# Folding a chunk's w_out with phi in the column group beside the logits' products, one chunk later

## The chip, the core and the metric

The kernel runs on one core of a Trainium2 chip. The metric is the device time of one execution in microseconds (us); the time of a kernel is the median of its runs.

## What is computed

Three layers follow each other: attention over 4 batches of 512 local and 32 global tokens (8 heads of 64), a gated feed-forward layer of 512 to 1536 to 512 (`moe_`), and a soft mixture of experts (`moe2_`). The change concerns the second layer's last matrix and the first product of the third:

```python
def _moe_ref(x, w_gate, w_val, w_out):
    g = x @ w_gate
    silu = g * (1.0 / (1.0 + np.exp(-g)))
    val = x @ w_val
    return silu * val @ w_out

def _moe2_ref(x, phi, w1, w2):
    logits = x @ phi
    d = softmax over the tokens; c = softmax over the slots
    slot_input = d.T @ x
    ...
```

The kernel never forms the second layer's output. With h = silu * val, the logits are h @ (w_out @ phi), so each 128 rows of w_out are multiplied with phi (512 x 32) once, and the 128 x 32 result is what the logits' products need.

## The kernel before, in words

The 17 tiles of 128 tokens (2176 tokens) are cut into blocks, and the blocks into two groups. Group 1 (`G1`) holds three blocks of 512 tokens, group 2 (`G2`) one of 384 and one of 256. The 1536 inner features are 12 chunks of 128 (`NFC` = 12). In group 1 the loop of line 847 goes over the chunks c, and in each over the three blocks: `gate(0, c, blk)` (line 605), then `val(0, c, blk)` (line 617). Each is one group of 12 TensorE products of 128 x 128 weights with 512 columns (`mm3`, line 594: four slices of x, three products each for the high and low parts). After a gate, ScalarE takes a tanh (line 612, tile `u`) and VectorE multiplies (line 613). After a val, VectorE multiplies again (line 622) and transposes (line 625). Between these, VectorE, ScalarE and GpSimd prepare the weights of the next chunk (lines 127 to 176).

Small pieces of work are put between the products by hand. `at(k, f)` (line 585) enters a piece f at step k, and `mm3` calls the pieces of a step after every third product. A chunk has `S1` = 24 steps: chunk c has the steps 24c to 24c + 23, its first gate the first four, its first val the next four, and so on. Pieces are issued in the engines' program order where they stand, so a piece on TensorE stands in front of all later products. The pieces of chunk c:

- `wprime(c)` (line 627) has three. Its `a` turns the chunk's 128 x 512 of w_out with four transposes into PSUM (`pwt`, line 634); ScalarE copies them out (`woT`, line 637). Its `b`, the fold, multiplies the four turned slices with the four slices of phi. Each of the four products gives 32 output rows, and they go to the four groups of 32 rows of `pwp` (line 642), one each, as four separate partial results. VectorE copies all 128 rows out (`ws`, line 647). Its `e`, the turn back, is one product `pws` (line 651) whose contraction over 128 rows with four stacked unit matrices (`istack`) adds the four partial results and turns them, to 128 x 32; ScalarE copies it out (`wp`, line 652).
- `logits_piece(0, [c - 1])` (line 656) has three products, one for each block: the folded weights of chunk c - 1 (128 x 32) with the block's `u` of 512 columns (line 669). Block 0, 1 and 2 write to output rows 0 to 31, 32 to 63 and 64 to 95 of one bank (`L`). Rows 96 to 127 stay free. They are added up over the chunks.

A product of 32 output rows uses one of four groups of 32 columns of TensorE's array, a product that contracts 32 rows one of four groups of 32 rows. The profile writes the part that an instruction uses as rows*columns: 128*128 is the whole array, 128*32 one column group, 32*128 one row group. A product of plain 32-bit floats is recorded as two MATMUL and two LDWEIGHTS, here called its two passes.

Before, the pieces stand at these steps of chunk c: the logits of chunk c - 1 at 5 (in the middle of the first val), `a` at 9, the fold at 12, the turn back at 15; for chunk 0 the three are five steps later. The `u` tiles live in two pools (line 793), one for even and one for odd chunks, of three buffers each. PSUM has three buffers for the groups of products (`ps_mm`), one for the transposes and one shared by `pwp` and `pws` (`ps_w`).

Of the kernel before, what the change touches and what calls it, by code (L numbers as in the profile page):

```python
# [23 lines left out]
NC = DM // P  # L24
# [12 lines left out]
def window(i):  # L37

    if i == 0:
        return 0, "A", 0  # L40
    m, k = divmod(i - 1, 3)
    return (4 * m, 4 * m + 2, 4 * m + 3)[k], "ABC"[k], m
# [3 lines left out]
def attention_moe_soft_moe_kernel(  # L46
# [15 lines left out]
    nc = tc.nc  # L62
    FF = w_gate.shape[1]
    NFC = FF // P
    NS = phi.shape[1]
# [19 lines left out]
    istack = cpool.tile([P, NS], F32, name="istack")  # L85
# [3 lines left out]
    phi_sb = cpool.tile([P, NC, NS], F32, name="phi_sb")  # L89
# [4 lines left out]
    for i, (_, n) in enumerate(BLOCKS):  # L94
        pool = x2pool if i in GROUPS[-1] else x1pool
        t = pool.tile([P, 2 * NC * n * P], F32R, name=f"x{i}")
        t = t.rearrange("p (a c n) -> p a c n", a=2, c=NC)
# [80 lines left out]
    def prep_some(n=1):  # L178
        for _ in range(min(n, len(prep))):
            prep.pop(0)()  # L180
# [86 lines left out]
    pw = ps_sc.tile([P, 512], F32, tag="sc", name="pw")  # L267
# [21 lines left out]
    for g in (0, 1, 3, 2):  # L289
# [7 lines left out]
        for r in range(3):  # L297
# [3 lines left out]
            k = window(first)[1]  # L301
# [277 lines left out]
    def cols(blk):  # L579
        return BLOCKS[blk][1] * P  # L580
# [4 lines left out]
    def at(k, f):  # L585
        plan.setdefault(k, []).append(f)
# [18 lines left out]
    def gate(g, c, blk, fill=True):  # L605
        n = cols(blk)
        pg = ps_mm.tile([P, 512], F32, tag="mm", name=f"pgate{g}_{c}_{blk}")
        mm3(pg, wchunk[c], 0, blk, fill)

        w, bufs = usize[c % 2]  # L610
        u = us[c, blk] = upools[c % 2].tile([P, w], F32, tag="u", name=f"u{g}_{c}_{blk}", bufs=bufs)
        nc.scalar.activation(u[:, :n], pg[:, :n], AF.Tanh, scale=0.5)  # L612
        nc.vector.scalar_tensor_tensor(  # L613
            out=u[:, :n], in0=u[:, :n], scalar=1.0, in1=pg[:, :n], op0=ALU.add, op1=ALU.mult
        )

    def val(g, c, blk, fill=True):
        n = cols(blk)
        pv = ps_mm.tile([P, 512], F32, tag="mm", name=f"pval{g}_{c}_{blk}")
        mm3(pv, wchunk[c], 1, blk, fill)  # L620
        u = us[c, blk]
        nc.vector.scalar_tensor_tensor(  # L622
            out=u[:, :n], in0=u[:, :n], scalar=0.5, in1=pv[:, :n], op0=ALU.mult, op1=ALU.mult
        )
        nc.vector.transpose(out=hT[blk][:, c], in_=u[:, :n])  # L625

    def wprime(c):

        d = {}

        def a():
            pt = ps_w.tile([P, NC, P], F32, tag="wt", name=f"pwt{c}")
            for cc in range(NC):
                nc.tensor.transpose(pt[:, cc], wo[c][:, cc * P : cc * P + P], ident)
            wo.pop(c)
            t = d["t"] = wtmp.tile([P, NC, P], F32, tag="woT", name=f"woT{c}")
            nc.scalar.activation(t, pt, AF.Copy)  # L637

        def b():
            pp = ps_w.tile([P, P], F32, tag="wp", name=f"pwp{c}")  # L640
            for j in range(NC):
                nc.tensor.matmul(
                    pp[32 * j : 32 * j + 32], phi_sb[:, j], d["t"][:, j],
                    start=True, stop=True, skip_group_check=True,
                )
            d["s"] = wtmp.tile([P, P], F32, tag="ws", name=f"ws{c}")
            nc.vector.tensor_copy(d["s"], pp)

        def e():
            pw = ps_w.tile([P, NS], F32, tag="wp", name=f"pws{c}")  # L650
            nc.tensor.matmul(pw, d["s"], istack, start=True, stop=True)
            nc.scalar.activation(wp[c], pw, AF.Copy)

        return a, b, e

    def logits_piece(g, cs, blks=None):

        group = GROUPS[g]
        per = 4 // len(group)

        def f():
            if g not in Lps:
                Lps[g] = ps_L.tile([P, 512], F32, tag="L", name=f"L{g}")
            for c in cs:
                for bi, blk in enumerate(group):
                    if blk not in (blks or group):
                        continue
                    cg, n = bi * per + c % per, cols(blk)
                    nc.tensor.matmul(  # L669
                        Lps[g][32 * cg : 32 * cg + 32, :n], wp[c], us.pop((c, blk))[:, :n],  # L670
                        start=(c < per), stop=(c >= NFC - per), skip_group_check=True,
                    )

        return f
# [164 lines left out]
    def w_fetch(i):  # L839
        c = i - NFC  # L840
        if c >= NFC:
            return
        w = wchunk[i] = ring_tile(i, f"wr{c}")
        nc.sync.dma_start(w.bitcast(F32), wkept[c])

    S1, S2 = 2 * NC * len(G1), 2 * NC * len(G2)
    for c in range(NFC):

        if c > 0:
            at(S1 * c + 5, logits_piece(0, [c - 1]))  # L850
        for k, f in zip((9, 12, 15), wprime(c)):
            at(S1 * c + k + (5 if c == 0 else 0), f)
        if c + 2 >= NFC:
            w_fetch(c + 2)
        for bi, blk in enumerate(G1):
            if c + 1 < NFC:
                w_prep(3 * (c + 1) + bi)
            if c > 0:
                gate(0, c, blk)
            prep_some(2)  # L860
            val(0, c, blk)
            prep_some(3)
# [34 lines left out]
    t = epool[0].tile([P, 4096], F32, name="dr0", tag="e0")  # L897
    t = [t[:, 512 * k : 512 * k + 512] for k in range(5)]
# [17 lines left out]
    k = base + 30  # L916
# [98 lines left out]
    d, a, b, top, turned, tokens, sums, NJ = part_end(2, Ls, [Ls], [place["rB"]])  # L1015
# [42 lines left out]
    t = dpool.tile([P, 4 * NF], F32, tag="Ts", name="sT")  # L1058
    nc.gpsimd.memset(t[:, : 5 * E * DG], 0.0)  # L1059
    t = t[:, : 5 * E * DG].rearrange("p (c k) -> p c k", c=5)  # L1060
# [5 lines left out]
    for h, hs in enumerate((H1, H2)):  # L1066
        psi = ps_mm.tile([P, DM // 2], F32, tag="mm", name=f"psi{h}")
        for c in range(NFC):
# [3 lines left out]
                start=(c < 4), stop=(c >= NFC - 4), skip_group_check=True,  # L1072
# [8 lines left out]
    for c in range(NC):  # L1081
        nc.tensor.matmul(
            psTi[:, c], (si0, si)[c // 2][:, c % 2 * P : c % 2 * P + P], istack,
            start=True, stop=True, skip_group_check=True,
# [48 lines left out]
    for k in range(3, 2 * E):  # L1133
# [4 lines left out]
        if side == 0:  # L1138
            t = epool[slot > 0].tile([P, 4096], F32, name=f"f{slot}", tag=f"e{slot}")
# [17 lines left out]
    for i in range(5, NEARLY):  # L1157
        t = epool[1].tile([P, 4096], F32, name=f"ob{i}", tag=f"e{i}")
# [121 lines left out]
```

## Time and profile before

| | |
|---|---|
| three runs | 537.39, 538.96, 540.86 us; median 538.96 |
| the profiled execution, its own time | 538.02 us |
| its span (first to last instruction) | 536.1 us |
| TensorE (PE) busy | 501.7 us, 94% of the span |
| VectorE (DVE), ScalarE (ACT), GpSimd (POOL) busy | 304.1, 181.8, 97.3 us |
| mean granted TensorE clock | 0.985 of full speed |

PE is TensorE's matmuls, PEld its weight loads, SP the engine that issues most transfers. A matmul's record is longer than the time to the next one's start, since they are pipelined: distances from start to start are what is read below. The lines of the tables belong to the program before; in the changed program the same code stands two or three lines lower from `wprime` on.

### The profile page before, as it was taken

The numbers are of one execution on the slowest core, as the hardware profiler recorded it, in microseconds if no ns is written. First come the engines' busy times: TensorE is split into PE (matmuls) and PEld (weight loads), VectorE is DVE, ScalarE is ACT, GpSimd is POOL, SyncE is SP. The second block draws the span as 40 slices with busy tenths as digits, with TensorE's granted clock in tenths as the row PEclk, the third lists the DMA queues.
The fourth block names the chain that finished last, engine by engine and source line by source line (L and its number), as shares of the span: only waits on it lengthen the run. The fifth ranks groups of instructions, "written<-read, shape, count | busy, mean of one in ns | idle before, by whom it ended". The sixth has DMA issues, their size and how long they took to land.

```text
span 536.1 us, 12836 instructions
## 1 busy us (share of the span) xinstructions
PE 501.7 (94%) x5274; PEld 373.9 (70%) x5274; DVE 304.1 (57%) x801; ACT 181.8 (34%) x550; POOL 97.3 (18%) x137
## 2 busy tenths in 40 slices
PE   5879999999999999999999999999999999779982
PEld 3668787887777777777777777785699997433631
DVE  7556988867776677677667666362243434521012
ACT  5758898873323223223223221130101112110011
POOL 7853665421201001001011110000000000100000
PEclk9899999999999999999999999999999999989997
DMA  8996886603653444344444463142199996869996
GB/s 217 303 272 179 234 265 166 172 5 98 216 174 122 163 150 156 138 137 158 137 150 168 141 231 134 43 158 81 60 398 384 415 388 205 320 211 351 348 360 194
DMA packets 61922, 109.94 MB, mean 205 GB/s; under 512 B 3752, under 2 KB 47784, under 8 KB 59944
## 3 DMA queue, kind: packets, MB, share of 16 engines
q1 hardware_dynamic: 61864, 109.13, 61.0%
q8 instruction: 41, 0.67, 0.5%
q14 instruction: 17, 0.14, 0.1%
HBM read 88.93 MB, written 20.19 MB: 204 GB/s over the span
## 4 chain that ended last, share of the span: by engine, by line
PE 70%; issue 13%; ACT 7%; DVE 4%; DMA 3%; SPq 1%; DVEq 0%; ACTq 0%
PE pval L598 22%; PE pgate L598 22%; PE sc L342 4%; PE ppT L372 3%; PE T L760 3%; PE psh L1101 3%; PE o L386 2%; DMA f<-in_w_dram 2%; ACT p L363 2%; PE pso L1171 2%; PE L L669 1%; PE gs L447 1%; SPq L876 1%; ACT woT L637 1%; PE pg L479 1%
## 5 line engine op out<-in xcount | busy, mean ns | idle before, releaser
L598 PE MATMUL pval<-x,w 128*128 128x512 f32 x432 | 112.3, 400 | 0.0
L598 PE MATMUL pgate<-x,w 128*128 128x512 f32 x432 | 109.8, 399 | 0.0
L598 PEld LDWEIGHTS pval<-x,w 128*128 128x128 f32 x432 | 79.4, 188 | 28.1 <-issue 11.6
L598 PEld LDWEIGHTS pgate<-x,w 128*128 128x128 f32 x432 | 79.5, 189 | 16.7
L613 DVE SCALAR_TENSOR_TENSOR u<-u,pgate 128x512 f32<-128x512 f32 (+2 forms) x60 | 36.5, 608 | 84.7 <-ACT u L612 84.6
L612 ACT ACTIVATE u<-pgate 128x512 f32<-128x512 f32 (+2 forms) x60 | 31.8, 530 | 128.3 <-PE pgate L598 106.5
L622 DVE SCALAR_TENSOR_TENSOR u<-u,pval 128x512 f32<-128x512 f32 (+2 forms) x60 | 36.4, 607 | 48.6 <-PE pval L598 48.5
L172 POOL TENSOR_TENSOR w<-wb,w 128x512 fp32r<-128x512 f32 x24 | 31.2, 1301 | 179.9 <-ACT w L171 179.8
L363 ACT ACTIVATE p<-sm,nm 128x128 f32<-128x128 f32 x128 | 49.4, 393 | 0.0
L598 PE MATMUL pgate<-x,wr 128*128 128x384 f32 (+1 forms) x288 | 49.3, 314 | 0.0
L598 PEld LDWEIGHTS pgate<-x,wr 128*128 128x128 f32 x288 | 43.5, 188 | 8.1 <-issue 7.4
L598 PE MATMUL pval<-x,wr 128*128 128x384 f32 (+1 forms) x288 | 48.5, 314 | 0.0
L598 PEld LDWEIGHTS pval<-x,wr 128*128 128x128 f32 x288 | 43.1, 189 | 7.0 <-issue 7.0
L171 ACT ACTIVATE w<-wb 128x512 fp32r<-128x512 f32 x24 | 15.2, 632 | 86.7 <-issue 51.4
L342 PE MATMUL sc<-kS,qB 128*64 128x128 f32 x512 | 34.0, 280 | 7.9 <-ACT pG L466 3.1
L342 PEld LDWEIGHTS sc<-kS,qB 128*64 128x64 f32 x512 | 28.4, 138 | 13.3 <-issue 8.2
L353 DVE CUSTOM_DVE_ANT_0 sm<-sc,masks 128x128 f32<-128x128 f32 x128 | 28.7, 286 | 11.0 <-PE sc L342 9.4
L157 DVE SCALAR_TENSOR_TENSOR wb<-wv,wb 128x512 f32<-128x512 f32 x36 | 25.6, 712 | 3.5
L1059 POOL MEMSET sT<- 128x1440 f32 x1 | 1.3, 1297 | 139.1 <-PE pTT L1038 139.1
L625 DVE STREAM_TRANSPOSE hT<-u 128x512 f32<-128x512 f32 x36 | 25.6, 712 | 1.3
L143 DVE SCALAR_TENSOR_TENSOR wb<-raw,wb 128x512 uint32<-128x512 uint32 x36 | 25.3, 704 | 1.1
L363 ACT ACTIVATION_READ_ACCUMULATOR p<-sm,nm 128x1 f32 x128 | 24.7, 193 | 0.0
(211 smaller groups left out, 679.3 us busy)
## 6 DMA issues: line engine op xcount, KB each, us to landing
e<-in_w_dram SPq DMA_DIRECT2D x7, 2048.0 KB, 12.8
w_d<-w SPq DMA_DIRECT2D x24, 512.0 KB, 2.6
wr<-w_d SPq DMA_DIRECT2D x12, 1024.0 KB, 6.2
f<-in_w_dram SPq DMA_DIRECT2D x10, 1024.0 KB, 12.0
raw<-in_wgate_dram SPq DMA_DIRECT2D x12, 512.0 KB, 3.6
raw<-in_wval_dram SPq DMA_DIRECT2D x12, 512.0 KB, 4.0
raw<-in_wout_dram SPq DMA_DIRECT2D x12, 512.0 KB, 3.5
kS<-in_kS_dram SPq DMA_DIRECT2D x7, 736.0 KB, 6.6
```

What stands on the lines that cost most here:

```text
L143: nc.vector.scalar_tensor_tensor(out=d["t"], in0=d["raw"][:, :, 0], scalar=29, in1=d["t"], op0=ALU.logical_shift_right, op1=ALU.bitwise_or,)
L157: nc.vector.scalar_tensor_tensor(out=w, in0=d["v"], scalar=F64_NORMAL, in1=w, op0=ALU.is_ge, op1=ALU.mult)
L172: nc.gpsimd.tensor_tensor(out=wl, in0=w, in1=wh, op=ALU.subtract)
L342: nc.tensor.matmul(sc[64 * (i % 2) : 64 * (i % 2) + 64, i // 2], qb[:, hp, blk], kS[n][:, hp, 32 * s0 : 32 * s0 + 128], start=True, stop=T ...
L353: nc.vector.tensor_tensor_reduce(out=sm[:, bp], in0=sc[:, bp], in1=masks[:, 4 * tp + bp], scale=-SCALE, scalar=3e38, op0=ALU.add, op1=ALU.min,
L363: nc.scalar.activation(d["p"][hp][:, bp], d["sm"][hp][:, bp], AF.Exp, bias=d["nm"][:, hp, bp : bp + 1], scale=-1.0, accum_out=d["rs"][:, b ...
L372: nc.tensor.transpose(pt[:, bp], d["p"][hp][:, bp], ident)
L598: nc.tensor.matmul(ps[:, :n], w[:, 2 * k + a, cc * P : cc * P + P], xt[b][:, cc], start=(cc == 0 and i == 0), stop=(cc == NC - 1 and i == 2),)
L612: nc.scalar.activation(u[:, :n], pg[:, :n], AF.Tanh, scale=0.5)
L613: nc.vector.scalar_tensor_tensor(out=u[:, :n], in0=u[:, :n], scalar=1.0, in1=pg[:, :n], op0=ALU.add, op1=ALU.mult)
L622: nc.vector.scalar_tensor_tensor(out=u[:, :n], in0=u[:, :n], scalar=0.5, in1=pv[:, :n], op0=ALU.mult, op1=ALU.mult)
L625: nc.vector.transpose(out=hT[blk][:, c], in_=u[:, :n])
```

## The change

```diff
@@ wprime
         def b():
+            r = slice(3 * NS, 4 * NS)
             pp = ps_w.tile([P, P], F32, tag="wp", name=f"pwp{c}")
             for j in range(NC):
                 nc.tensor.matmul(
-                    pp[32 * j : 32 * j + 32], phi_sb[:, j], d["t"][:, j],
-                    start=True, stop=True, skip_group_check=True,
+                    pp[r], phi_sb[:, j], d["t"][:, j],
+                    start=(j == 0), stop=(j == NC - 1), skip_group_check=True,
                 )
             d["s"] = wtmp.tile([P, P], F32, tag="ws", name=f"ws{c}")
-            nc.vector.tensor_copy(d["s"], pp)
+            nc.vector.tensor_copy(d["s"][r], pp[r])
 
         def e():
+            r = slice(3 * NS, 4 * NS)
             pw = ps_w.tile([P, NS], F32, tag="wp", name=f"pws{c}")
-            nc.tensor.matmul(pw, d["s"], istack, start=True, stop=True)
+            nc.tensor.matmul(pw, d["s"][r], istack[r], start=True, stop=True)
             nc.scalar.activation(wp[c], pw, AF.Copy)
@@ the loop over the chunks of group 1
+        last = c == NFC - 1
+        f, fold, back = wprime(c)
+        at(S1 * c + (14 if c == 0 else 9), f)
+        k = S1 * c + 13 if last else S1 * (c + 1) + 3
         if c > 0:
-            at(S1 * c + 5, logits_piece(0, [c - 1]))
-        for k, f in zip((9, 12, 15), wprime(c)):
-            at(S1 * c + k + (5 if c == 0 else 0), f)
+            at(k, logits_piece(0, [c - 1]))
+        at(k, fold)
+        at(k + 4, back)
```

The fold's four products now all write to output rows 96 to 127, the group that the logits' products leave free, and add up there, one after the other. VectorE copies 32 rows instead of 128. The turn back contracts those 32 rows alone, in one row group. The transposes stay where they were. The fold of chunk c moves to step 3 of chunk c + 1, right behind the logits of chunk c - 1, which also go there (before: step 5 of chunk c); the turn back follows at step 7. The last chunk has its logits (of chunk 10), fold and turn back at its own steps 13, 13 and 17. In chunk 1 the fold of chunk 0 stands alone, with no logits before it. The number of products is the same.

On TensorE, from the first gate of chunk 2 to its last: `pgate_2_0` is the gate of chunk 2, block 0. Before:

```order
L598 MATMUL pgate_2_0_2792<-x_82,w_2686 128x512 x12
L598 MATMUL pval_2_0_2813<-x_82,w_2686 128x512 x6
L669 MATMUL L_2670<-u_1_0_2655,wp_2533 32x512
L669 MATMUL L_2670<-u_1_1_2711,wp_2533 32x512
L669 MATMUL L_2670<-u_1_2_2764,wp_2533 32x512
L598 MATMUL pval_2_0_2813<-x_82,w_2686 128x512 x6
L598 MATMUL pgate_2_1_2840<-x_83,w_2686 128x512 x6
L634 MATMUL pwt_2847<-ident,wb_2767 128x128 x4
L598 MATMUL pgate_2_1_2840<-x_83,w_2686 128x512 x6
L598 MATMUL pval_2_1_2868<-x_83,w_2686 128x512 x3
L642 MATMUL pwp_2872<-woT_2852,phi_sb 32x128 x4
...
L651 MATMUL pws_2888<-istack,ws_2877 128x32
```

The same stretch of the changed program:

```order
L598 MATMUL pgate_2_0_2778<-x_82,w_2682 128x512 x12
L672 MATMUL L_2791<-u_0_0_2357,wp_2532 32x512
L672 MATMUL L_2791<-u_0_1_2472,wp_2532 32x512
L672 MATMUL L_2791<-u_0_2_2501,wp_2532 32x512
L644 MATMUL pwp_2795<-woT_2699,phi_sb 32x128 x4
L598 MATMUL pval_2_0_2810<-x_82,w_2682 128x512 x12
L654 MATMUL pws_2823<-istack,ws_2800 128x32
L598 MATMUL pgate_2_1_2837<-x_83,w_2682 128x512 x6
L634 MATMUL pwt_2844<-ident,wb_2753 128x128 x4
L598 MATMUL pgate_2_1_2837<-x_83,w_2682 128x512 x6
L598 MATMUL pval_2_1_2865<-x_83,w_2682 128x512 x12
```

The logits' three products and the fold's four now stand in one place between the first gate and the first val, the logits those of two chunks ago; the turn back stands behind the first val.

On VectorE, around the first gate of chunk 3 (`wb` are the weights in preparation, `ws` is the fold's copy). Before:

```order
L157 SCALAR_TENSOR_TENSOR wb_2916<-wv_2917,wb_2916 128x512
L613 SCALAR_TENSOR_TENSOR u_3_0_2954<-u_3_0_2954,pgate_3_0_2941 128x512
L137 TENSOR_SCALAR wb_2957<-raw_2894 128x512
L143 SCALAR_TENSOR_TENSOR wb_2957<-raw_2894,wb_2957 128x512
L622 SCALAR_TENSOR_TENSOR u_3_0_2954<-u_3_0_2954,pval_3_0_2962 128x512
```

After:

```order
L157 SCALAR_TENSOR_TENSOR wb_2903<-wv_2904,wb_2903 128x512
L649 COPY ws_2949<-pwp_2944 32x128
L613 SCALAR_TENSOR_TENSOR u_3_0_2951<-u_3_0_2951,pgate_3_0_2928 128x512
L137 TENSOR_SCALAR wb_2954<-raw_2881 128x512
L143 SCALAR_TENSOR_TENSOR wb_2954<-raw_2881,wb_2954 128x512
L622 SCALAR_TENSOR_TENSOR u_3_0_2951<-u_3_0_2951,pval_3_0_2959 128x512
```

The copy, which stood in front of the line 622 of block 1, now stands in front of the line 613 of block 0. The orders of GpSimd and of the transfers are the same as before.

## Rows read from the trace of the kernel before

**Rows 1.** The page, part 4: the chain that ended last, shares by engine.
```profile
PE 70%; issue 13%; ACT 7%; DVE 4%; DMA 3%; SPq 1%; DVEq 0%; ACTq 0%
```

**Rows 2.** Stretch, its us, busy us (instructions) of PE, PEld, DVE, ACT, POOL; clock, DMA, GB/s.
```profile
146.20:352.00 205.80, 204.02 (x986) 151.99 (x986) 136.88 (x224) 52.87 (x104) 25.44 (x20) 1.00 0.43 149
```

**Rows 3.** Timeline of PE, chunk 4: start us, us, line, out<-in, count [idle <-releaser].
```profile
196.11 1.56 PE L598 MATMUL pval<-x,w 128*128 128x512 f32 x6
197.60 1.06 PE L669 MATMUL L<-u,wp 128*32 128x512 f32 x6
198.59 1.67 PE L598 MATMUL pval<-x,w 128*128 128x512 f32 x6
200.10 1.55 PE L598 MATMUL pgate<-x,w 128*128 128x512 f32 x6
...
203.32 0.86 PE L598 MATMUL pval<-x,w 128*128 128x512 f32 x3
204.36 0.43 PE L642 MATMUL pwp<-woT,phi_sb 128*32 128x128 f32 x8 [0.18 <-ACT woT L637]
...
206.92 0.32 PE L651 MATMUL pws<-istack,ws 128*128 128x32 f32 x2
207.08 3.04 PE L598 MATMUL pgate<-x,w 128*128 128x512 f32 x12
209.95 2.96 PE L598 MATMUL pval<-x,w 128*128 128x512 f32 x12
212.75 2.96 PE L598 MATMUL pgate<-x,w 128*128 128x512 f32 x12
215.55 1.57 PE L598 MATMUL pval<-x,w 128*128 128x512 f32 x6
```

**Rows 4.** The same timeline, chunk 0 and chunk 11.
```profile
127.85 2.33 PE L598 MATMUL pval<-x,w 128*128 128x512 f32 x9
...
135.34 2.95 PE L598 MATMUL pgate<-x,w 128*128 128x512 f32 x12
...
338.89 0.86 PE L598 MATMUL pval<-x,w 128*128 128x512 f32 x3
...
345.24 2.96 PE L598 MATMUL pval<-x,w 128*128 128x512 f32 x12
```

**Rows 5.** Who waited for whom on PE, 126 to 352 us: total us, times, longest.
```profile
PE pwp L642 <- ACT woT L637: 1.7, 9, 0.2
```

**Rows 6.** Timeline of PE in the attention: one unit's scores.
```profile
62.68 1.09 PE L342 MATMUL sc<-kS,qB 128*64 128x128 f32 x16
```

**Rows 7.** Line 342 (the scores): ns min/median/max, first and last start, shape.
```profile
L342 PE MATMUL sc<-kS,qB x512: 269/273/418, 6.7 to 109.5; 128*64 128x128 f32 x171
```

**Rows 8.** Line 669 (logits, group 2), records under way between 394.62 and 394.65 us.
```profile
L669 PE MATMUL L<-u,wp x6: 380/404/510, 394.4 to 394.6; 128*32 128x256 f32 x4, 128*32 128x384 f32 x2
```

**Rows 9.** Timeline around a product with 64 contracted rows (line 707), PE.
```profile
446.83 0.88 PE L598 MATMUL pval<-x,wr 128*128 128x256 f32 x6
447.63 0.91 PE L707 MATMUL LB<-xa,istack 64*128 64x384 f32 x2
448.47 0.64 PE L598 MATMUL pval<-x,wr 128*128 128x256 f32 x3
448.95 0.52 PE L598 MATMUL pgate<-x,wr 128*128 128x256 f32 x3
```

**Rows 10.** The chain in order of time: start us, us; a group of 256 columns.
```profile
427.76 1.43 PE pgate L598 x12
```

**Rows 11.** Timeline of DVE around the first gate of chunk 5.
```profile
215.06 0.69 DVE L157 SCALAR_TENSOR_TENSOR wb<-wv,wb 128x512 f32<-128x512 f32 x1
216.38 0.69 DVE L613 SCALAR_TENSOR_TENSOR u<-u,pgate 128x512 f32<-128x512 f32 x1 [0.62 <-ACT u L612]
...
219.73 0.69 DVE L622 SCALAR_TENSOR_TENSOR u<-u,pval 128x512 f32<-128x512 f32 x1 [1.59 <-PE pval L598]
```

**Rows 12.** Timeline of ACT at the same place.
```profile
215.75 0.60 ACT L612 ACTIVATE u<-pgate 128x512 f32<-128x512 f32 x1 [4.12 <-PE pgate L598]
```

## The prediction

> **What bounds the kernel now.** I read the chain of waits first, by engine: 70% of the span is TensorE [rows 1]. In a table of stretches, group 1 from chunk 1 on (146.2 to 352 us) has TensorE busy 204.0 of 205.8 us at the full granted clock, 1.00 of 2.4 GHz, while VectorE is busy 137 and ScalarE 53 [rows 2]. So in this stretch time is the sum of what TensorE issues; other engines matter only where TensorE waits for them. In the list of who waited for whom, TensorE waits for one thing there: the fold for ScalarE's copy of the transposes, 1.7 us in nine places [rows 5].
>
> Then the timeline of one chunk. A group of 12 products with nothing between them takes 2.80 us from start to start (209.95 to 212.75, and 212.75 to 215.55), 0.233 a product [rows 3]. Each piece put between products costs what its group takes beyond that:
> - the logits: 196.11 to 200.10 is 3.99, so 1.19 us;
> - fold and turn back: the 24 products from 203.32 to 209.95 take 6.63 against 5.60, so 1.03 us. Of this the turn back is 0.23: 0.16 from 206.92 to 207.08, and 0.07 by which the next group is longer than 2.80. The fold is the other 0.80, with its wait of 0.18.
>
> **What is removed.** Nine chunks fold with such a wait, so 9 x 1.03 = 9.3 us. Chunk 11 has none: 24 products from 338.89 to 345.24 take 6.35, so 0.75 [rows 4]. Chunk 0 takes 7.49 for the 27 products from 127.85 to 135.34, 1.19 over 6.30; about 0.1 of that I leave to the transposes just ahead, so 1.1. Chunk 1, not shown, I put between, at 1.0. Sum 12.1 us. The transposes and the logits' own 1.19 us stay, whatever their step: both places interrupt the same stream.
>
> **What is added: the fold beside the logits.** Do the fold's eight passes run while the logits' six do? The scores of the attention show how a chain runs in one column group: 16 passes of 128 columns, eight in each of two groups of 64 columns, stand in 1.09 us [rows 6]. A record lasts 0.27 [rows 7], so the last starts 0.82 after the first: 0.117 a pass, and eight of them 0.94 us, with the other group's eight beside them. That column groups also keep their own pace is seen where logits of 384 and of 256 columns stand together: at 394.62 to 394.65 all four passes of 256 columns have begun, but only two of the four with 384 [rows 8]; the short ones' second passes did not wait for the long ones' first. From the logits' first start to the next product are 0.99 us (197.60 to 198.59) [rows 3]. The fold, issued seventh some hundredths later, needs 0.94 plus the way out, so it sticks out by 0 to 0.07; I take 0.04. Eleven places, 0.4 us.
>
> In chunk 1 the fold of chunk 0 stands alone, in one column group: 0.94 for its passes. What entering and leaving another form of tile costs I read at a product that contracts 64 rows [rows 9], against 0.119 a product of 256 columns there (1.43 for 12) [rows 10]. It begins 0.09 late (446.83 plus six products is 447.54, it starts at 447.63); from its start to the next product are 0.84, of which its two passes of 384 columns take some 0.68 (six times 0.117 is 0.70, a little less without the first weights); and the three products behind take 0.48 instead of 0.36, 0.12 more. So 0.09 + 0.16 + 0.12 = 0.37 beside the streaming. The lone fold costs 0.94 + about 0.3 = 1.2 us.
>
> **What is added: the turn back in a row group.** Today it uses the whole array like its neighbours and costs 0.23. With 32 contracted rows it is a tile of another form than the products on both sides, and no row shows such a product with so few columns. From below: 0.37 for changing form twice plus two passes of 32 columns, a quarter of 0.117 each, is 0.43. From above: 0.37 plus all that it costs today is 0.60. I take 0.54, nearer the upper end, since its second weights of 128 columns cannot be covered by a pass as short as 0.03, as the second weights of the 384-column pass can. Twelve times 0.54 is 6.5 us, bounds 5.2 to 7.2.
>
> The Trainium skill, "TensorEngine Tiling (Array Packing)", Key Properties, says that a change of tiling mode drains TensorE. By that rule the turn back gets dearer by the change, and the trace agrees: 0.09 in and 0.12 out at [rows 9]. Without it the turn back would stay at 0.23, a rival below.
>
> **What hides the rest.** VectorE's copy of the fold: at the first gate of chunk 5 VectorE has finished its weight preparation at 215.75 and waits until 216.38 for the tanh [rows 11]. After the change the logits and fold start where that gate ends, about 215.6, and end near 216.6; the copy follows by about 217.0, and the turn back comes behind the next 12 products, at about 219.4. Margin some 2.4 us. The wait also queues behind the copy on VectorE the multiplication of line 613, which waits for the tanh anyway. The tanh (215.75 to 216.35 [rows 12]) must now wait until the logits have read its buffer, so it starts near 216.6, 0.9 later, and line 613 with it; the val's multiplication that follows on VectorE today waits 1.59 for TensorE [rows 11], which takes this up. The PSUM buffer that line 613 frees is wanted again two groups later, over 5 us. If these covers failed, each us would count twelve times. The transposes' copy, for which the fold waits today, is now 18 of a chunk's 24 steps old, some 14 us: that wait goes, and nothing else is late there. No transfer moves, on no queue. Everything behind group 1 is started by TensorE's progress, so I let the whole gain pass to the end.
>
> **Sum.** 0.4 + 1.2 + 6.5 = 8.1 added, 12.1 removed: 4.0 us less. The profiled execution took 538.02 (span 536.1 and 1.9 around it); it becomes 534.0. It is 0.9 below the median of the runs; from the median, 538.96 - 4.0 = 534.9 us, 0.75% less. By the bounds (0 to 0.8 for the overhang, 5.2 to 7.2 for the turn back, 0.2 either way elsewhere) the gain is 2.9 to 5.9, so 533.1 to 536.1.
>
> **Rivals.**
> - *The fold's chain runs behind the logits, not beside them.* All these products use all 128 rows, and the fold is issued last; if its weights had to wait for the logits' products, each of eleven places would pay 0.94 instead of 0.04, 9.9 us more: 534.9 + 9.9 = 544.8, slower. It turns the sign once the fold sticks out by 0.40 (4.0/11 + 0.04). Against it are the independent groups of [rows 6, 8]; for it, that no row shows two lengths of chain. 0.08. In the Trainium skill, "TensorE: Matmul & The Clock Gate", Part 3, weights overlap running products only where the row groups differ; here they don't differ, and by that rule this rival would be the forecast. In [rows 8] second passes start under running ones of the same rows, which is against the rule.
> - *The turn back costs no change of form*, and stays at 0.23: 12 x 0.31 = 3.7 more gained, 531.2. Against it speak [rows 9], though they have 64 rows and long passes. 0.12.
> - *VectorE or ScalarE comes late*, so that the turn back waits half a us in each chunk: +6.0, 540.9. It would need 2.4 us of margin to vanish. 0.05.
> - *The gain is lost behind group 1*, in the last stage's transfers, which TensorE also waits for: 538.5 to 539, no change. The transfers are issued as TensorE frees their buffers, which speaks against it. 0.07.
> - The forecast: 0.68.
>
> **How the numbers follow.** A measurement of this kernel tells about 1%, 5.4 us, from no change. The forecast lies below that; with its bounds and the scatter of the medians (the three runs span 3.5 us) a fifth of it falls over 1% faster: 0.14, and nearly all of the second rival, 0.11: faster 0.25. Slower by over 1% takes 0.05 of the first rival and 0.01 of the third: 0.06. The rest, 0.69, is within 1%. The range of 530.5 to 539.5 holds the forecast, the second and the fourth rival, and leaves out the first and part of the third. The forecast's own range is 533 to 536.5.
>
> **What would show it.** In the timeline after: the logits and the fold side by side, about 1.0 us from the first logits' start to the next product in chunks 2 to 11, near 1.9 if the first rival holds; a lone fold of 0.9 in chunk 1; the turn back delaying TensorE by some 0.54, against 0.23; no wait of the fold for ScalarE; chunk to chunk 19.0 us instead of 19.4 (196.11 to 215.55 [rows 3]). The forecast is wrong if a new wait for VectorE stands before the turn back, or if group 1 ends 4 us sooner and the last instruction does not.

## The result, and the profile after

The changed kernel takes 532.80 us (median of 8 runs, 530.85 to 536.16) against 538.64 (8 runs, 536.88 to 540.86): a ratio of 0.989, 95% interval 0.986 to 0.993, 5.8 us less. A second set of 7 runs gave 532.49 and 0.991 (0.988 to 0.994). The forecast was 534.9 and 0.75% less, in a range of 530.5 to 539.5.

TensorE sets the end as before. The chain of the page after, by engine, the line that answers to [rows 1]:

```profile
PE 88%; DVE 4%; ACT 4%; issue 2%; DVEq 0%; ACTq 0%
```

The 18 points more of TensorE have two sources. In this execution the chain did not pass through the last transfers; in the second trace of the same kernel it did, and there TensorE has 80%. The rest is the share called issue, 2% here and 3% there, against 13% before [rows 1]. Most of that 13% was nine stretches like this one, in which the chain before left TensorE from the logits to the fold of a chunk and came back by way of ScalarE's copy `woT`:

```profile
197.46 5.72 issue
```

What the change did stands in the timeline of TensorE. Chunk 4 after (columns as in [rows 3]; here its first gate, the logits of chunk 2 with the fold of chunk 3, its first val, the turn back):

```profile
188.91 2.96 PE L598 MATMUL pgate<-x,w 128*128 128x512 f32 x12
191.80 0.63 PE L672 MATMUL L<-u,wp 128*32 128x512 f32 x3
191.82 0.62 PE L644 MATMUL pwp<-woT,phi_sb 128*32 128x128 f32 x4
192.25 0.60 PE L672 MATMUL L<-u,wp 128*32 128x512 f32 x3
192.28 0.60 PE L644 MATMUL pwp<-woT,phi_sb 128*32 128x128 f32 x4
192.81 3.05 PE L598 MATMUL pval<-x,w 128*128 128x512 f32 x12
195.79 0.40 PE L654 MATMUL pws<-istack,ws 32*128 32x32 f32 x2
196.12 1.67 PE L598 MATMUL pgate<-x,w 128*128 128x512 f32 x6
197.63 0.60 PE L634 MATMUL pwt<-ident,wb 128*128 128x128 f32 x4
```

The logits' first three passes start at 191.80 and the first of the fold's at 191.82; the logits' second passes follow at 192.25, while the fold goes on beside them, and the next product starts at 192.81, 1.01 us after the first logits. Before, with the logits alone, it was 0.99 [rows 3]. Seven of the fold's eight weight loads stand under the running products (PEld, the same place):

```profile
191.85 0.76 PEld L644 LDWEIGHTS pwp<-woT,phi_sb 128*32 128x32 f32 x7
```

The turn back is now 32*128 and has 0.33 us to the next product, 0.16 before. From this chunk's first gate to the next one's are 18.95 us (188.91 to 207.86), 19.43 before (193.32 to 212.75). The list of who waited for whom has no row for TensorE between 126 and 350 us: the wait of [rows 5] is gone and none has come.

How long group 1 lasts from its first transposes to the first gate of group 2, before (with two plain groups of 12 products):

```profile
127.49 0.60 PE L634 MATMUL pwt<-ident,wb 128*128 128x128 f32 x4
...
190.59 2.89 PE L598 MATMUL pval<-x,w 128*128 128x512 f32 x12
193.32 2.95 PE L598 MATMUL pgate<-x,w 128*128 128x512 f32 x12
...
348.04 2.26 PE L598 MATMUL pgate<-x,wr 128*128 128x384 f32 x12
```

and after (with the lone fold in chunk 1):

```profile
125.82 0.60 PE L634 MATMUL pwt<-ident,wb 128*128 128x128 f32 x4
...
135.33 1.06 PE L644 MATMUL pwp<-woT,phi_sb 128*32 128x128 f32 x8
136.32 3.07 PE L598 MATMUL pval<-x,w 128*128 128x512 f32 x12
...
341.47 2.27 PE L598 MATMUL pgate<-x,wr 128*128 128x384 f32 x12
```

That is 348.04 - 127.49 = 220.55 before, 341.47 - 125.82 = 215.65 after: 4.9 us less, 0.9%. All stages, from the first starts of such products in the traces (lines as in the kernel before; the table below takes group 1 in the same way for every run):

| us | to the first gate (attention) | to the first transposes | group 1 | group 2, to its first product of 64 rows on line 707 | to line 1070 | to line 1101 | to line 1146 | to the end |
|---|---|---|---|---|---|---|---|---|
| before | 113.0 | 14.5 | 220.5 | 99.6 | 25.6 | 5.7 | 14.5 | 42.6 |
| before, two more traces | 114.4, 112.0 | 14.5 | 220.5, 220.5 | 99.6 | 27.2, 27.0 | 5.3, 5.5 | 14.5 | 41.8, 42.8 |
| after | 111.4 | 14.5 | 215.65 | 99.6 | 26.5 | 6.0 | 14.5 | 41.5 |
| after, second trace | 112.6 | 14.5 | 215.65 | 99.6 | 26.4 | 5.9 | 14.5 | 41.9 |

Group 1 and its two neighbours repeat to 0.06 us; the attention and most of the stages behind group 2 do not, and carry the scatter of the runs.

### The profile page after: what moved, and what is told of

It reads as the page before. It is cut to its first block, busy times and chain, and to the rows that moved or that the text cites. A ratio compares the mean times of both kernels' runs of the same rounds, so it can differ in the third digit from the quotient of the medians.

```text
span 529.5 us, 12845 instructions
## 1 busy us (share of the span) xinstructions
PE 499.8 (94%) x5274; PEld 382.9 (72%) x5274; DVE 306.3 (58%) x801; ACT 181.9 (34%) x550; POOL 97.6 (18%) x137
## 4 chain that ended last, share of the span: by engine, by line
PE 88%; DVE 4%; ACT 4%; issue 2%; DVEq 0%; ACTq 0%
PE pgate L598 28%; PE pval L598 27%; PE sc L342 5%; PE ppT L372 3%; PE pso L1180 3%; PE T L763 3%; PE o L386 3%; PE psh L1110 3%; PE L L672 2%; PE pwp L644 2%; ACT p L363 2%; PE pg L479 1%; PE psh L1017 1%; PE gs L447 1%; PE pxT L421 1%
## 5 line engine op out<-in xcount | busy, mean ns | idle before, releaser
L598 PE MATMUL pval<-x,w 128*128 128x512 f32 x432 | 107.1, 396 | 0.0
L342 PEld LDWEIGHTS sc<-kS,qB 128*64 128x64 f32 x512 | 29.6, 142 | 12.8 <-issue 7.2
L157 DVE SCALAR_TENSOR_TENSOR wb<-wv,wb 128x512 f32<-128x512 f32 x36 | 25.6, 712 | 3.5
L625 DVE STREAM_TRANSPOSE hT<-u 128x512 f32<-128x512 f32 x36 | 25.6, 712 | 1.3
```

The source lines that it names most:

```text
L157: nc.vector.scalar_tensor_tensor(out=w, in0=d["v"], scalar=F64_NORMAL, in1=w, op0=ALU.is_ge, op1=ALU.mult)
L342: nc.tensor.matmul(sc[64 * (i % 2) : 64 * (i % 2) + 64, i // 2], qb[:, hp, blk], kS[n][:, hp, 32 * s0 : 32 * s0 + 128], start=True, stop=T ...
L598: nc.tensor.matmul(ps[:, :n], w[:, 2 * k + a, cc * P : cc * P + P], xt[b][:, cc], start=(cc == 0 and i == 0), stop=(cc == NC - 1 and i == 2),)
```

## The experiments

Group 1's length, as above, is what the variants are compared by; the medians carry the scatter of the other stages as well. Each ratio is to runs of the kernel before that were taken beside the variant (median 538.65 for e1 to e4, 538.07 for e5 to e7).

What a piece costs TensorE is the distance from the start of the product before it to the start of the fourth product behind it, less four plain distances; the plain distance is the mean of all distances under 0.25 us between neighbouring products of group 1 (the longer ones stand right behind a piece), 0.2315 us before and 0.2314 after. So read, the places of the changed kernel cost in the mean 1.21 us for logits and fold (the logits alone, before: 1.19), 0.53 for the turn back and 1.21 for the lone fold.

| kernel | group 1, us | median, us | ratio to before (95%) |
|---|---|---|---|
| before | 220.5 | 538.64 | 1 |
| changed | 215.65 | 532.80 | 0.989 (0.986 to 0.993) |
| changed, again (e6) | 215.65 | 532.49 | 0.991 (0.988 to 0.994) |
| e1, turn back over the whole array | 211.96 | 529.91 | 0.984 (0.981 to 0.987) |
| e2, moved, four column groups | 213.44 | 530.55 | 0.986 (0.983 to 0.990) |
| e3, fold ahead of the logits | 220.53 | 538.51 | 1.000 (0.997 to 1.003) |
| e4, fold three products later | 229.06 | 547.91 | 1.014 (1.009 to 1.020) |
| e5, e1 with a lone fold in four groups | 211.22 | 529.06 | 0.985 (0.981 to 0.988) |
| e7, turn back at once | 222.46 | 540.03 | 1.005 (1.002 to 1.008) |

**e4: does the gain need both side by side?**

```diff
-        at(k, fold)
+        at(k + 1, fold)
```

> The changed kernel with the fold one step, three products, behind the logits, so that nothing runs beside it. Theory (the gain needs both side by side; a lone chain of eight passes in one column group costs the 1.20 us that chunk 1's does): 11 x 1.18 = 13 us over the changed kernel, near 546, ratio 1.013. Rival (what the change saves is the wait for ScalarE, and a fold without wait costs the 0.56 of the kernel before): about 6 us over the changed kernel, near 539.

It took 547.91; group 1 is 13.4 us longer than in the changed kernel, as the theory had it.

```profile
198.27 1.06 PE L672 MATMUL L<-u,wp 128*32 128x512 f32 x6
199.26 0.97 PE L598 MATMUL pval<-x,w 128*128 128x512 f32 x3
200.16 1.06 PE L644 MATMUL pwp<-woT,phi_sb 128*32 128x128 f32 x8
201.15 2.38 PE L598 MATMUL pval<-x,w 128*128 128x512 f32 x9
```

From the fold's start to the next product are 201.15 - 200.16 = 0.99 us, for which the same chain in the changed kernel adds 0.02. So a fold in one column group pays only beside the logits: alone it costs 1.2 us, more than the old one in four with its wait (0.80). This does not yet say that the one column group is better beside the logits than four; that is e2's question.

**e3: does the order within the place matter?**

```diff
+        at(k, fold)
         if c > 0:
             at(k, logits_piece(0, [c - 1]))
-        at(k, fold)
```

> The changed kernel with the fold issued ahead of the logits at the same step. Theory (products are issued in order and a column group takes the next product only when it has room for its weights, so the logits wait until the last of the fold's four products is taken in, and then the column groups run beside each other for the rest only): each of eleven places some 0.5 to 0.7 us longer, about 6 to 7 us over the changed kernel, near 539.5, ratio 1.0. Rival (column groups take their work independently of the order): no difference from the changed kernel, 532.8.

It took 538.51: the whole gain is lost, by nothing but the order of seven products.

```profile
192.97 0.73 PE L644 MATMUL pwp<-woT,phi_sb 128*32 128x128 f32 x5
193.43 0.63 PE L672 MATMUL L<-u,wp 128*32 128x512 f32 x3
193.53 0.49 PE L644 MATMUL pwp<-woT,phi_sb 128*32 128x128 f32 x3
193.88 0.60 PE L672 MATMUL L<-u,wp 128*32 128x512 f32 x3
194.42 3.04 PE L598 MATMUL pval<-x,w 128*128 128x512 f32 x12
```

The fold starts at 192.97, the logits only at 193.43, when five of the fold's eight passes have started; from the first start to the next product are 1.45 us against 1.01. The lost 0.44 times eleven is 4.8, and group 1 is 4.9 longer. I had put 0.5 to 0.7 a place; the direction was right, the size a little high. The weight loads at the same place show where the logits stood:

```profile
192.96 0.57 PEld L644 LDWEIGHTS pwp<-woT,phi_sb 128*32 128x32 f32 x6 [0.37 <-issue]
193.43 0.15 PEld L672 LDWEIGHTS L<-u,wp 128*32 128x32 f32 x6
193.54 0.22 PEld L644 LDWEIGHTS pwp<-woT,phi_sb 128*32 128x32 f32 x2
```

The logits' weights come behind six of the fold's eight loads and ahead of those of its last product. So the logits were held back although their three column groups had nothing to do, and not until the fold's last weights were loaded. That they waited until its last product was taken in, with its weights still to come, fits this; it is my reading, and no run shows it by itself.

**e2: what is the move worth without the new column group?**

```diff
-                    pp[r], phi_sb[:, j], d["t"][:, j],
-                    start=(j == 0), stop=(j == NC - 1), skip_group_check=True,
+                    pp[32 * j : 32 * j + 32], phi_sb[:, j], d["t"][:, j],
+                    start=True, stop=True, skip_group_check=True,
...
-            nc.vector.tensor_copy(d["s"][r], pp[r])
+            nc.vector.tensor_copy(d["s"], pp)
...
-            nc.tensor.matmul(pw, d["s"][r], istack[r], start=True, stop=True)
+            nc.tensor.matmul(pw, d["s"], istack, start=True, stop=True)
```

> The move without the new column group: the pieces stand at the steps of the changed kernel, but the fold gives four partial results in four column groups as before, VectorE copies 128 rows, the turn back contracts 128. Theory (three of the four products now queue behind the logits in their own column groups, two passes of 128 columns each, so the fold sticks out by about 0.24 us in eleven places instead of 0.02; the turn back is 0.25 instead of 0.53, the lone fold 0.56 instead of 1.20): +2.4 - 3.4 - 0.6 = 1.6 us under the changed kernel, near 531.2, ratio 0.986. Rival (the gain of the change comes from the free column group): the fold costs 0.56 in each place and only its waits are gone, about 536, ratio 0.995.

It took 530.55, group 1 2.2 us under the changed kernel's. The rival, 536, fell.

```profile
195.44 0.63 PE L672 MATMUL L<-u,wp 128*32 128x512 f32 x3
195.48 0.41 PE L644 MATMUL pwp<-woT,phi_sb 128*32 128x128 f32 x2
195.89 0.61 PE L672 MATMUL L<-u,wp 128*32 128x512 f32 x3
196.32 0.40 PE L644 MATMUL pwp<-woT,phi_sb 128*32 128x128 f32 x6
196.64 3.05 PE L598 MATMUL pval<-x,w 128*128 128x512 f32 x12
```

Two of the fold's passes, those of the fourth group, start at 195.48 beside the logits; the other six start at 196.32, behind the logits' second passes in the same column groups. The place takes 1.20 us instead of 1.01. It is 0.19 dearer in eleven places, 2.1 in all, but its turn back (0.22 of TensorE, against 0.53) and its lone fold (0.56 against 1.21) give back 3.7 and 0.6. So the sum is -2.2, as measured. Beside the logits the column group is worth 2.1 us; the changed kernel pays more than that for the narrower turn back that came with it. The theory had 0.24 us a place instead of 0.02, which is 2.4 in all, and so put this kernel 1.6 us under the changed one.

**e1: is it the form of the tile that makes the turn back dear?**

```diff
-            d["s"] = wtmp.tile([P, P], F32, tag="ws", name=f"ws{c}")
+            if "ws" not in held:
+                held["ws"] = wtmp.tile([P, P], F32, tag="ws", name="ws")
+                nc.gpsimd.memset(held["ws"], 0.0)
+            d["s"] = held["ws"]
...
-            nc.tensor.matmul(pw, d["s"][r], istack[r], start=True, stop=True)
+            nc.tensor.matmul(pw, d["s"], istack, start=True, stop=True)
```

> The changed kernel, but the turn back contracts all 128 rows again: the copied tile is set to zero once, so the rows other than 96 to 127 add nothing. The turn back then has the same form of tile as its neighbours. Theory (the change of form costs 0.53 - 0.25 = 0.28 us at each of 12 turn backs): about 3.4 us under the changed kernel, near 529.5, ratio to before 0.983. Rival (the turn back is dearer because it comes close behind VectorE's copy, or for its place): no difference from the changed kernel, 532.8, ratio 0.989.

It took 529.91; group 1 is 3.7 us shorter than in the changed kernel, 0.31 a turn back.

```profile
196.76 3.05 PE L598 MATMUL pval<-x,w 128*128 128x512 f32 x12
199.65 0.30 PE L659 MATMUL pws<-istack,ws 128*128 128x32 f32 x2
199.79 1.64 PE L598 MATMUL pgate<-x,w 128*128 128x512 f32 x6
```

From the turn back to the next product 199.79 - 199.65 = 0.14 us instead of 0.33, and the way in and out is shorter too: from the start of the val to that of the gate 3.03 us for 12 products, against 196.12 - 192.81 = 3.31. The weight loads of the turn back, in the changed kernel and in e1:

```profile
195.79 0.29 PEld L654 LDWEIGHTS pws<-istack,ws 32*128 32x128 f32 x2 [0.36 <-issue]
199.43 0.41 PEld L659 LDWEIGHTS pws<-istack,ws 128*128 128x128 f32 x2
```

In e1 they start at 199.43, 0.22 before its first pass and under val's last product; in the changed kernel only at 195.79, with the first pass. The place is the same, and TensorE waits for no engine in either; the form has changed.

Both e1 and e2 turn back over the whole array, so the two compare the column group by itself: 213.44 - 211.96 = 1.5 us, which is the 2.1 of eleven places less the 0.6 of the lone fold.

**e5: both improvements.** To e1, chunk 0's fold goes to four column groups and a tile of its own, all else as there.

```diff
+                o = slice(32 * j, 32 * j + 32) if c == 0 else r
                 nc.tensor.matmul(
-                    pp[r], phi_sb[:, j], d["t"][:, j],
-                    start=(j == 0), stop=(j == NC - 1), skip_group_check=True,
+                    pp[o], phi_sb[:, j], d["t"][:, j],
+                    start=(c == 0 or j == 0), stop=(c == 0 or j == NC - 1), skip_group_check=True,
                 )
+            if c == 0:
+                d["s"] = wtmp.tile([P, P], F32, tag="ws0", name="ws0")
+                nc.vector.tensor_copy(d["s"], pp)
+                return
```

> The kernel of e1 (turn back over the whole array), with chunk 0's lone fold in four column groups as in the kernel before, since nothing runs beside it. Theory: the lone fold 0.56 instead of 1.20, so 0.64 us under e1 (529.9), near 529.3, ratio 0.983; in the trace group 1, from the first transposes to the first gate of group 2, 211.3 us against 212.0 in e1. Rival (a fold of four column groups is dearer in this place, through VectorE's copy of 128 rows): no difference from e1.

Group 1 is 211.22, 0.74 under e1, as expected within 0.1.

```profile
139.12 0.43 PE L647 MATMUL pwp<-woT,phi_sb 128*32 128x128 f32 x8
139.48 3.04 PE L598 MATMUL pval<-x,w 128*128 128x512 f32 x12
```

The lone fold has 0.36 us to the next product, 0.99 in the changed kernel (135.33 to 136.32). The median of 529.06 and the ratio of 0.985 cannot be told from e1's, but the trace can: it is the shortest group 1 of all, 9.3 us under the kernel before.

**e7: what does the cover of VectorE's copy hide?**

```diff
-        at(k + 4, back)
+        at(k, back)
```

> The changed kernel with the turn back right behind the fold, at the same step, so that no products cover VectorE's copy. Theory (the copy ends 0.6 us after the fold, 193.31 against 192.71 at one place of the changed kernel, and the waiting turn back holds up the products behind it on TensorE; one way out and in, some 0.2 us, is saved): 12 times 0.55 to 0.7 us, 6.5 to 8.5 over the changed kernel, near 540, ratio 1.003. Rival (the turn back waits little, since VectorE is free): no difference, 532.8.

It took 540.03; group 1 is 6.8 us longer than in the changed kernel. The waits of TensorE in group 1 (total us, times, longest):

```profile
PE pws L654 <- DVE ws L649: 6.6, 12, 1.6
```

and one such place in its timeline:

```profile
197.61 0.60 PE L644 MATMUL pwp<-woT,phi_sb 128*32 128x128 f32 x4
198.67 0.40 PE L654 MATMUL pws<-istack,ws 32*128 32x32 f32 x2 [0.45 <-DVE ws L649]
199.00 3.06 PE L598 MATMUL pval<-x,w 128*128 128x512 f32 x12
201.89 1.56 PE L598 MATMUL pgate<-x,w 128*128 128x512 f32 x6
```

The turn back now waits 0.45 for the copy, and val's products stand behind it. So it is in eleven of the twelve places; the twelfth, in chunk 1, where the copy queues on VectorE behind the preparation of weights, is another matter:

```profile
139.58 0.40 PE L654 MATMUL pws<-istack,ws 32*128 32x32 f32 x2 [1.59 <-DVE ws L649]
139.92 4.61 PE L598 MATMUL pval<-x,w 128*128 128x512 f32 x12
144.37 1.57 PE L598 MATMUL pgate<-x,w 128*128 128x512 f32 x6
```

Its wait is 1.59, and behind it val takes 4.45 us to the next gate, against 2.89 at the place above (199.00 to 201.89). The row of 139.90 to 144.40 (as in [rows 2]) has a granted clock of 0.62:

```profile
139.90:144.40 4.50, 4.50 (x14) 3.53 (x14) 1.72 (x3) 1.25 (x3) 0.00 (x0) 0.62 0.61 178
```

After that idle time TensorE ran most of this stretch at the lower of its two clocks, 1.2 GHz, and lost 1.56 us by it; in the changed kernel the clock is 1.00 there. So 1.59 + 1.56 = 3.15 of the 6.8 us come from one place, and the other eleven give some 3.6, 0.33 each: the wait of 0.45 less what is saved on a way out and in. That is below the 0.55 to 0.7 of the theory, and that the sum fell into its range is luck. That the cover the prediction counted on was needed, and is enough where it stands, is shown. In the changed kernel the copy on VectorE:

```profile
191.55 0.69 DVE L157 SCALAR_TENSOR_TENSOR wb<-wv,wb 128x512 f32<-128x512 f32 x1
193.01 0.30 DVE L649 COPY ws<-pwp 32x128 f32<-32x128 f32 x1 [0.76 <-PE pwp L644]
193.51 0.69 DVE L613 SCALAR_TENSOR_TENSOR u<-u,pgate 128x512 f32<-128x512 f32 x1 [0.21 <-ACT u L612]
...
195.90 0.69 DVE L622 SCALAR_TENSOR_TENSOR u<-u,pval 128x512 f32<-128x512 f32 x1 [0.63 <-PE pval L598]
```

It ends at 193.31, 2.5 us before the turn back at 195.79. The tanh on ScalarE, held up by the logits and fold:

```profile
192.88 0.60 ACT L612 ACTIVATE u<-pgate 128x512 f32<-128x512 f32 x1 [4.70 <-PE pwp L644]
```

It starts at 192.88 and the multiplication of line 613 at 193.51, and the val's multiplication at 195.90 still waits 0.63 for TensorE: the delay is taken up, as forecast.

**e6, e8 and e9: is anything gained outside group 1?** e6 is the changed kernel again, e8 and e9 the kernel before.

> The changed kernel once more, for its own scatter. Theory (the change is worth the 4.9 us that group 1 lost in the trace, and the rest of the 5.8 between the medians is scatter of the attention and of the last stage): ratio 0.991, about 533.7, group 1 within 0.2 us of 215.65. Rival (the change also shortens another stage): ratio 0.989 again, and a stage other than group 1 shorter than before by the same amount as in the first trace of the changed kernel.

> The kernel before once more, for its trace: in the first trace its last stage (from the turning of the experts' hidden layer to the end) is 42.6 us, in the traces of the changed kernel and its variants 41.5 to 42.0. Theory (scatter of the transfers in the last stage): 41.5 to 42.6, group 1 at 220.5 again. Rival (the change shortens the last stage as well, by about 0.9): 42.6 again.

> The same kernel before, a second trace. The same two answers: 41.5 to 42.6 for scatter, 42.6 again for an effect of the change on the last stage.

The group 1 of e6 is 215.65 to the hundredth, and those of e8 and e9 220.5. The last stage took 42.6, 41.8 and 42.8 in the kernel before and 41.5 and 41.9 in the changed one: the two overlap. All eight traces of the changed kernel and its variants lie at 41.5 to 41.9, so a small effect there is not excluded. From the end of group 1 to the end of the program nothing of it is left: 188.1, 188.4 and 189.3 us before, 188.0 and 188.3 after. The attention, which the change does not touch, took 111.4 to 116.2 over the traces of all runs. So 4.9 of the 5.8 us between the medians are shown to be the change; the other 0.9 lie within the interval and were not traced to anything.

## Why the prediction was right

- *TensorE alone sets group 1, and a piece costs what it delays the products.* Right. Group 1 lost 4.9 us and the stage behind it kept its 99.6 us; the rest of the program, 188 to 189 us before and 188 after, shows neither a gain of its own nor a loss. The rival of a gain lost behind group 1 fell.
- *The fold runs beside the logits and sticks out by 0.04 us* (bounds 0 to 0.07): measured 0.02, eleven times. The rival that it runs behind them fell in the first trace, and e4 shows what it would have cost. The fold's products of all 128 rows begin at 191.82, and seven of their eight weight loads stand from 191.85 on, under the logits' products of the same rows. The page of the Trainium skill that spoke for the rival ("TensorE: Matmul & The Clock Gate", Part 3: weights overlap running products only in other row groups) does not hold here.
- *The lone fold 1.2 us*: 0.99 to the next product, with the way in and out 1.21.
- *The turn back 0.54*, chosen between bounds of 0.43 and 0.60: measured 0.53. e1 shows that the form is the reason; that the choice met it to 0.01 is partly luck. The rival that the change of form costs nothing fell. The Trainium skill's rule, "TensorEngine Tiling (Array Packing)", Key Properties, that a change of tiling mode drains TensorE, agrees with e1's 0.31 us a turn back.
- *The covers.* Right: 2.5 us of margin for the copy where I had 2.4, and the late tanh delays no product. e7 shows that the first was needed.
- *The sum, 4.0 us*: group 1 gave 4.9. The mis-sized term is what is removed. I took 2.80 us for a plain group of 12 from two at the end of chunk 4 and the start of chunk 5; in other chunks plain groups take 2.72 or 2.73 as well (193.32 - 190.59 above). With the mean distance of 0.2315 us, 2.78 a group, fold and turn back together cost 12.55 us in the twelve chunks before, not 12.1. The overhang gives some 0.15 more (0.02 instead of 0.04, eleven times), the turn back 0.15. Together 4.75; the last 0.1 lies in the plain products themselves (0.2314 instead of 0.2315, over 800 of them).
- *The range.* The bounds of the gain, 2.9 to 5.9, hold the 4.9. By the prediction's own terms the lower one is 2.7: the 0.2 either way was added above and left out below. The median of 532.80 is 2.1 under the forecast and 0.2 under the forecast's own range of 533 to 536.5. Of the 2.1, 0.9 is group 1, 0.3 the lower median of the kernel before, and 0.9 was not traced to anything.
- *No difference that a measurement tells*, within 1%, was the likeliest case, at 0.69, with 0.25 for faster by over 1%. The medians came out at 1.1% (0.7 to 1.4 by the interval), a second set at 0.9%: the true size lies at the border, and the runs do not decide on which side.

## What to carry to other kernels

Where TensorE is full, count each small piece of work as the time by which it delays the stream: its way in, its longest chain in one column group, its way out. A chain in a column group that nobody else needs was all but free here beside longer products (0.02 us) when issued behind them, and cost 0.44 us more when issued ahead. The turn back should have kept the form of its neighbours, even with rows of zeros to contract: 32 rows instead of 128 cost here 0.31 us more, not less. The runs give the parts of the 4.9 us: the move by itself 7.1 (e2 against the kernel before), the column group 1.5 (e1 against e2), the narrow turn back -3.7 (the changed kernel against e1). So the change lost more by the narrow turn back than it took from the column group: e1 and e5, with one zeroed tile, are 3.7 and 4.4 us shorter in group 1.

## What the runs showed that I had not expected

The price of order. The prediction put the fold behind the logits and gave no thought to the other order; e3, expected to lose the gain, lost all of it by issuing the short chain first. With the fold behind, products later in the program start before passes of earlier ones: in chunk 4 four passes of the fold, two whole products, start from 191.82 on, before the logits' second passes at 192.25. In e2 the fold's fourth product starts 0.84 us ahead of its first three (195.48 and 196.32); VectorE's copy of all four still starts behind them, at 196.79. Taken together I read e2 and e3 so: each column group works through its own products in order, but new work is given out in the program's order, and a product that finds no room holds up those behind it. No run tests this reading alone.

And the move by itself was worth more than the column group: e2, with the old four partial results and the old turn back, beats the changed kernel by 2.2 us of group 1. With a shared entry and exit and without the wait for ScalarE, it loses only 0.19 us a place by its longer overhang, and its turn back is the cheap one.
